# Attention with a linear feed-forward: the products of probabilities and values, key blocks in another order

## The chip, the cores and the metric

The kernel runs on one core of a Trainium2 chip. TensorE (PE) multiplies, VectorE (DVE) and ScalarE (ACT) work on what it leaves in PSUM, GpSimd (POOL) does little here, and SyncE (SP) issues DMAs. The metric is the device time of one execution in microseconds (us); lower is better.

## The reference

Attention over 4 batches, 8 heads, 768 positions and heads of 64, followed by a feed-forward without a nonlinearity:

```python
scores = scale * np.matmul(q, k.transpose(0, 1, 3, 2))
keep = is_global | is_local        # key < 8, or 0 <= query - key < 96
scores = np.where(keep, scores + bias, -1000000000.0)
a = np.exp(scores - np.max(scores, axis=-1, keepdims=True))
a = a / (np.sum(a, axis=-1, keepdims=True) + 1e-09)
attn = np.matmul(a, v)
...
h = (x @ w1) * (x @ w2) @ w3       # x: attn, heads side by side
out = h @ w_out
```

A query sees the 8 first keys and the 96 behind it, so the scores are a narrow band.

## The kernel before, in words

The attention part goes in 24 steps of 128 queries of one batch (`s`), for all eight heads at once, and two steps make a pair (`d`, 12 of them, three to a batch). Within a step the queries are cut into four groups of 32 (`R`); four pairs of heads (`hp`) lie at 32 rows each. For a step, PE multiplies queries and keys into `sc` in PSUM (`scores`, L963), DVE adds the bias and takes the maximum (`maxima`), ACT takes exponentials (`exponentials`), DVE divides by the sums (`scale_part`) and transposes the probabilities into `pt` (`turn`, L1013). The transposes of the even step of a pair come first, then those of the odd one, in the early pairs in one piece for each step, later in two halves.

When both steps of a pair are there, `values(d)` (L1016 to 1027) multiplies the probabilities with the values (`vr`). It goes over key blocks `i` of 32 keys, 12 for a pair (9 where the pair begins a batch, since the first three would lie before the batch). A key block meets the query groups whose band holds it: blocks 0 to 11 meet 1, 2, 3, 4, 5, 5, 5, 5, 4, 3, 2, 1 groups of 32 queries, so the products have 32 to 160 columns. A block has 8 products, one for each head: four pairs of heads in four groups of 32 rows of the array, and two heads of a pair in two groups of 64 columns. All is in float32, and each product is two weight loads (of the 32 x 64 values) and two matmuls on PE, which the profile counts apart. All blocks of a pair add into the same place in `sc`. `start` is set on the first block and `stop` on the last.

Blocks 0 to 3 read only probabilities of the even step of the pair, block 4 is the first to read the odd step's first group, block 6 the first that needs the odd step's second half.

The order of PE's work is the order in which the code issues it. The first eight steps stand in a list written out by hand (`ORDER`, V.0 to V.3 are `values(0)` to `values(3)`), the rest in `planned` and the loop behind it, which lays pieces of the feed-forward (the list `plan`) between the pieces of attention; `values(d)` is called there whole, but for pair 10, which is called in two pieces, blocks 0 to 7 and 8 to 11 (`CUT`). So a stage of values is a closed run on PE, with feed-forward matmuls before and behind it. The feed-forward goes on for 130 us after the last pair, in split products of seven multiplications.

Of the kernel before, what the change touches and what calls it, by code (L numbers as in the profile page):

```python
# [30 lines left out]
R = 32  # L31
NR = P // R
# [5 lines left out]
NB = S // P  # L38
NV = 3 * NR
# [19 lines left out]
PREPARED = (3, 1), (3, 5), (3, 6), (3, 2), (3, 7), (3, 4), (6, 1), (6, 5), (6, 6), (6, 7), (7, 1), (7, 5), (6, 4)  # L59
WIDE_AT = (2, 4), (2, 5), (2, 6), (2, 7), (3, 0), (3, 4), (3, 5)  # L60
CUT = 8
SHARED = 12
QUIET = 18, 104
LATER, HELD = (15,), (18,)
# [745 lines left out]
def strided(ap, *dims):  # L810

    return bass.AP(ap.tensor, ap.offset, [ap.ap[0], *dims])
# [15 lines left out]
def banded(ctx, tc, ff, ns, nt, n1, nf, oki, qk, vx, sc, pr):  # L828


    nc = tc.nc
# [23 lines left out]
    late, masked = [], []  # L855
# [109 lines left out]
    def maxima(s, q):  # L965

        if q == 0:
            stats[s] = [at.tile([P, NR, 2], F32, tag=t, bufs=2, name=f"{t}_{s}") for t in ("mx", "sm")]
        w0, w1 = frame(s, q)
        for u in range(2):  # L970
            bias = (biasw if s % NB else bias0)[:, u, q, w0:w1]
            nc.vector.tensor_tensor_reduce(out=pr[:, q, u, GLB + w0:GLB + w1], in0=scored(s, u, q, w0, w1), in1=bias, scale=-SCALE, scalar=3.0e38, op0=ALU.add, op1=ALU.min, accum_out=stats[s][0][:, q, u:u + 1])  # L972
# [42 lines left out]
    def values(d, first=0, end=NV):  # L1015


        pt, v = pts[d], vrs[d]
        i0 = 0 if d % (NB // 2) else NR - 1
        for i in range(max(i0, first), end):  # L1020
            n0, n1 = max(0, i - NR), min(2 * NR, i + 1)
            for hp in range(NP):
                rows = slice(hp * R, (hp + 1) * R)
                for u in range(2):
                    cols = slice(u * D, (u + 1) * D)
                    turned = strided(pt[rows, i * P + u * PF + n0 * (2 * PF - P):], [2 * PF - P, n1 - n0], [1, R])
                    nc.tensor.matmul(sc[cols, hp, n0 * R:n1 * R], lhsT=v[rows, i, cols], rhs=turned, start=i == i0, stop=i == NV - 1, skip_group_check=True)  # L1027

# [144 lines left out]

    units, homes, later, raws = {}, {}, {}, []
    do = dict(pj=ff.join, bo=ff.blocks_out, ps=ff.combine, sh=ff.sums_high, sl=ff.sums_low, so=ff.sums_out, A=lambda *x: ff.convert(0, *x), B=lambda *x: ff.convert(1, *x), C=lambda *x: ff.convert(2, *x), wh=ff.high, wl=ff.low, F=ff.fold, Y=lambda f: ff.fold_first(f, sc), ye=lambda f: ff.fold_begun(f, sc), ya=ff.fold_sum, pe=ff.fold_out, ph=ff.fold_high, pl=ff.fold_low, S=scores, R=maxima, E=exponentials, s=sums, c=lambda s: scale(s, nc.scalar if s in BY_ROWS else nc.vector), X=turn, V=values, h=high, l=low, bias=distances, bD=masks, bE=globals_near, biasA=biases, nt=sizes)
    do.update((name, lambda *x, method=method: getattr(units[0], method)(*x)) for name, method in (("U", "first"), ("a", "gate"), ("g", "product"), ("gh", "high"), ("gl", "low"), ("Z", "second"), ("ot", "store")))

# [113 lines left out]
    with tc.manual_schedule(engines={mybir.EngineType.PE}):  # L1293
        with tc.manual_schedule(engines={mybir.EngineType.DVE, mybir.EngineType.SP, mybir.EngineType.Activation, mybir.EngineType.Pool}):
            ordered()
        with tc.manual_schedule(engines={mybir.EngineType.Activation, mybir.EngineType.DVE}):
# [6 lines left out]
            def go(until):  # L1303
                for _, *todo in plan[done[0]:until]:
                    (_, call, *x), *rest = todo
                    call(*x)
                    for call, x in waiting:
                        call(*x)
                    waiting.clear()
                    for late, call, *x in rest:  # L1310
                        if late:
                            waiting.append((call, x))
                        else:
                            call(*x)
                done[0] = max(done[0], until)
                if done[0] == len(plan):
                    for call, x in waiting:
                        call(*x)
                    waiting.clear()

            def on(k):
                go(done[0] + k)

            def rows(s, paces, begun=False):
                if not begun:
                    maxima(s, 0)
                    if s >= SHARED:
                        on(1)
# [35 lines left out]
            for d in range(STEPS // 2, PAIRED):  # L1364
                load(d)
                for s in (2 * d + 2, 2 * d + 3):
                    keys(s)
                for s in (2 * d, 2 * d + 1):
                    rows(s, (1,) * NR)
                    first = d % 2 == 0 and s % 2 == 0  # L1370
                    on(2 if first else 0 if s % 2 else 3)
                    rest(s, 2 if first else 1)
                    if s % 2 == 0:
                        on(1 if first else 2)
                go(place["Z", 1, 2, 6] if d % 2 else place["U", 1, 4, 1, 1])
                values(d)
                tokens(d)
                go(place["Z", 1, 3, 2] if d % 2 else place["Z", 1, 0, 0])
                scores(2 * d + 2)
                scores(2 * d + 3)  # L1380
            start = place["Z", 1, 3, 2]
            with tc.manual_schedule(engines={mybir.EngineType.SP}):
# [5 lines left out]
                for d in range(PAIRED, n // 2):  # L1388
                    when, cut, gap = MEET[d][:3]
                    for s in (2 * d, 2 * d + 1):  # L1390
                        rows(s, MEET[d][3 + s % 2], s % 2 == 1)
                        on(1)

                        def middle():
                            if d > PAIRED and s % 2 == 0:
                                scores(s + 1)
                                if d < n // 2 - 1:
                                    keys(s + 3)

                        shared(s, middle)  # L1400
                        if s % 2 == 0:
                            on(1)
                    go(start + when)
                    values(d, 0, CUT if cut else NV)
                    if cut:
                        on(cut)
                        values(d, CUT)
                    if d < n // 2 - 1:
                        load(d + 1)
                    ff.release()  # L1410
                    tokens(d)
                    go(start + when + cut + gap)
                    if d < n // 2 - 1:
                        scores(2 * d + 2)
                        if d < n // 2 - 2:
                            keys(2 * d + 4)
# [44 lines left out]
```

## Time and profile before

| | |
|---|---|
| median of 3 runs | 503.88 us (503.84 to 504.58) |
| the profiled execution | 504.05 us, span 502.3 us |
| PE busy (matmuls) | 496.8 us, 99% of the span |
| DVE, ACT busy | 378.5 us (75%), 250.9 us (50%) |
| granted TensorE clock | 1.00 |
| line 1027 (the change's matmuls) | 2112 matmuls, from 47.0 to 372.0 us |

A matmul's end is modelled in the profile and runs over the next one's start, so a busy PE can still have gaps in its streaming. The time of a stage is read from its first matmul to the first matmul of what follows. The number behind an x in a stretch of the profile counts every matmul or weight load that is under way somewhere in the stretch; with a stretch that begins just before a stage, it is the number that have started up to the stretch's end.

### The profile page before, as it was taken

How to read it: one execution, taken by the hardware profiler on the slowest of the kernel's cores; microseconds unless marked ns; L12 is line 12 of the kernel's file. 1: busy time of each engine (PE TensorE's matmuls, PEld its weight loads, DVE VectorE, ACT ScalarE, POOL GpSimd, SP SyncE). 2: the span in 40 equal slices, each digit the busy share in tenths (PEclk: the TensorE clock that was granted, in tenths of full speed). 3: DMA queues.
4: the chain of work that ended last, by engine and by line, in shares of the span. 5: the costliest groups of instructions: out<-in, count | busy, mean ns of one | idle time of the engine just before them, and what ended most of it. 6: DMA issues, size and time to landing. Idle time of an engine off the chain costs nothing.

```text
span 502.3 us, 14240 instructions
## 1 busy us (share of the span) xinstructions
PE 496.8 (99%) x5920; PEld 407.3 (81%) x5920; DVE 378.5 (75%) x941; ACT 250.9 (50%) x730; POOL 3.8 (1%) x29
## 2 busy tenths in 40 slices
PE   8999999999999999999999999999999999999997
PEld 5445568888888888889999889999888888888997
DVE  7999989999997984958585757685867566367971
ACT  7148637454544543548474757564654211243641
POOL 3000000000000000000000000000000000000000
PEclk9999999999999999999999999999999999999999
DMA  8997906994869979468582346691112764000112
GB/s 314 417 369 286 386 22 198 374 346 145 309 205 383 301 246 350 159 228 269 211 330 67 124 135 221 194 404 57 60 44 77 206 199 127 21 2 0 43 44 89
DMA packets 39498, 99.96 MB, mean 199 GB/s; under 512 B 3458, under 2 KB 22658, under 8 KB 38274
## 3 DMA queue, kind: packets, MB, share of 16 engines
q1 hardware_dynamic: 39280, 98.84, 56.2%
q8 instruction: 48, 0.79, 0.6%
q14 instruction: 24, 0.20, 0.1%
q10 hardware_dynamic: 146, 0.13, 0.1%
HBM read 75.89 MB, written 23.07 MB: 197 GB/s over the span
## 4 chain that ended last, share of the span: by engine, by line
PE 98%; DVE 1%; ACT 0%; issue 0%; ACTq 0%
PE x L436 18%; PE y L436 11%; PE w L288 11%; PE o L369 7%; PE o L371 7%; PE o L370 7%; PE sc L1027 6%; PE m L336 6%; PE m L338 6%; PE m L337 6%; PE sc L963 4%; PE oy L636 3%; PE ox L636 2%; PE sc L436 2%; PE sc L636 1%; PE sc L296 1%
## 5 line engine op out<-in xcount | busy, mean ns | idle before, releaser
L979 ACT ACTIVATE pr<-pr,mx 128x136 f32<-128x136 f32 (+2 forms) x192 | 74.6, 391 | 35.2 <-DVE mx L972 35.0
L461 ACT ACTIVATE ag<-x 128x256 f32<-128x256 f32 (+1 forms) x48 | 21.8, 453 | 67.0 <-PE x L436 61.8
L369 PE MATMUL o<-wh,gh 128*128 128x512 f32 x128 | 51.4, 401 | 0.0
L371 PE MATMUL o<-wh,gl 128*128 128x512 f32 x128 | 50.0, 390 | 0.0
L370 PE MATMUL o<-wl,gh 128*128 128x512 f32 x128 | 49.9, 390 | 0.0
L336 PE MATMUL m<-xh,w12h 128*128 128x512 f32 x112 | 43.9, 392 | 0.0
L338 PE MATMUL m<-xh,w12l 128*128 128x512 f32 x112 | 43.6, 389 | 0.0
L337 PE MATMUL m<-xl,w12h 128*128 128x512 f32 x112 | 43.6, 389 | 0.0
L972 DVE CUSTOM_DVE_ANT_0 pr<-sc,biasw 128x136 f32<-128x136 f32 x144 | 34.7, 294 | 6.2 <-PE sc L963 5.1
L1013 DVE STREAM_TRANSPOSE pt<-pr 128x640 f32<-128x640 f32 (+1 forms) x37 | 38.3, 1037 | 0.6
L979 ACT ACTIVATION_READ_ACCUMULATOR pr<-pr,mx 128x1 f32 x192 | 36.3, 189 | 0.0
L1027 PEld LDWEIGHTS sc<-pt,vr 32*64 32x64 f32 x2112 | 30.6, 130 | 4.4 <-issue 1.8
L436 PE MATMUL x<-xh,w12h 128*128 128x256 f32 (+1 forms) x152 | 33.5, 302 | 0.0
L436 PE MATMUL x<-xh,w12l 128*128 128x256 f32 (+1 forms) x152 | 33.3, 301 | 0.0
L1027 PE MATMUL sc<-pt,vr 32*64 32x160 f32 (+4 forms) x2112 | 32.4, 266 | 0.0
L288 PE MATMUL w<-wo,kt 128*128 128x512 f32 x64 | 28.4, 597 | 0.9 <-DVE wo L208 0.9
L436 PE MATMUL x<-xl,w12l 128*128 128x256 f32 (+1 forms) x96 | 29.2, 318 | 0.0
L436 PE MATMUL x<-xl,w12h 128*128 128x256 f32 (+1 forms) x96 | 29.2, 318 | 0.0
L369 PEld LDWEIGHTS o<-wh,gh 128*128 128x128 f32 x128 | 24.0, 188 | 5.8 <-issue 0.8
L371 PEld LDWEIGHTS o<-wh,gl 128*128 128x128 f32 x128 | 24.0, 188 | 5.3
L436 PEld LDWEIGHTS x<-xh,w12h 128*128 128x128 f32 x152 | 26.1, 190 | 1.8 <-issue 0.4
L370 PEld LDWEIGHTS o<-wl,gh 128*128 128x128 f32 x128 | 24.1, 188 | 4.1
(287 smaller groups left out, 1134.4 us busy)
## 6 DMA issues: line engine op xcount, KB each, us to landing
qr<-qk SPq DMA_DIRECT2D x20, 720.0 KB, 6.9
w12h<-ws SPq DMA_DIRECT2D x16, 512.0 KB, 5.7
w12l<-ws SPq DMA_DIRECT2D x16, 512.0 KB, 5.8
vr<-vx SPq DMA_DIRECT2D x8, 768.0 KB, 4.8
w12h<-ws SPq DMA_DIRECT2D x8, 768.0 KB, 6.2
w12l<-ws SPq DMA_DIRECT2D x8, 768.0 KB, 7.4
out_dram<-ot SPq DMA_DIRECT2D x19, 256.0 KB, 2.4
raws<-w SPq DMA_DIRECT2D x4, 1024.0 KB, 7.8
```

The lines of the kernel that those rows point to most:

```text
L288: self.nc.tensor.matmul(self.prod[f], lhsT=block.bitcast(F32), rhs=self.wo[:, k].bitcast(F32), start=first, stop=k == NFC - 1)
L336: self.nc.tensor.matmul(ps, lhsT=mh, rhs=xh[:, i], start=i == 0, stop=False)
L337: self.nc.tensor.matmul(ps, lhsT=mh, rhs=xl[:, i], start=False, stop=False)
L338: self.nc.tensor.matmul(ps, lhsT=ml, rhs=xh[:, i], start=False, stop=i == NCC - 1)
L369: self.nc.tensor.matmul(ps, lhsT=gh, rhs=ff.wh[:, f], start=f == first, stop=False)
L370: self.nc.tensor.matmul(ps, lhsT=gh, rhs=ff.wl[f], start=False, stop=False)
L371: self.nc.tensor.matmul(ps, lhsT=gl, rhs=ff.wh[:, f], start=False, stop=f == last)
L436: self.nc.tensor.matmul(out, lhsT=w[:, i], rhs=x[:, i], start=fresh and i == 0 and j == 0, stop=i == 1 and j == 2, skip_group_check=True)
L972: nc.vector.tensor_tensor_reduce(out=pr[:, q, u, GLB + w0:GLB + w1], in0=scored(s, u, q, w0, w1), in1=bias, scale=-SCALE, scalar=3.0e38, o ...
L979: nc.scalar.activation(x, x, AF.Exp, bias=mx[:, q, u:u + 1], scale=-1.0, accum_out=sm[:, q, u:u + 1])
L1013: nc.vector.transpose(strided(pts[d][:, (half * NR + q0) * 2 * PF:], [PF, 2 * (q1 - q0)], [P, NR + 1], [1, R]), x.rearrange("p n (k c) -> ...
L1027: nc.tensor.matmul(sc[cols, hp, n0 * R:n1 * R], lhsT=v[rows, i, cols], rhs=turned, start=i == i0, stop=i == NV - 1, skip_group_check=True)
```

## The change

The key blocks of a pair are visited in an order that is written out, one for full pairs, one for the pairs that begin a batch, and one for pair 4 (`LATE_TURN`). In widths (units of 32 columns) they are 5 1 5 2 4 3 5 1 5 2 4 3 for full pairs, 4 5 5 5 1 5 2 4 3 for those that begin a batch, and 4 1 3 2 5 5 5 1 5 2 4 3 for pair 4. Pair 10, which is cut, has 5 1 5 2 4 3 5 5 and then 1 2 4 3. `start` and `stop` follow the first and the last block of the order.

```diff
+LATE_TURN = 4
+ORDERS = {"full": (4, 0, 5, 1, 3, 2, 6, 11, 7, 10, 8, 9), "late": (3, 0, 2, 1, 4, 5, 6, 11, 7, 10, 8, 9), "first": (3, 4, 5, 6, 11, 7, 10, 8, 9)}
...
         pt, v = pts[d], vrs[d]
-        i0 = 0 if d % (NB // 2) else NR - 1
-        for i in range(max(i0, first), end):
+        order = [i for i in ORDERS["first" if d % (NB // 2) == 0 else "late" if d == LATE_TURN else "full"] if first <= i < end]
+        for i in order:
             n0, n1 = max(0, i - NR), min(2 * NR, i + 1)
...
-                    nc.tensor.matmul(sc[cols, hp, n0 * R:n1 * R], lhsT=v[rows, i, cols], rhs=turned, start=i == i0, stop=i == NV - 1, skip_group_check=True)
+                    nc.tensor.matmul(sc[cols, hp, n0 * R:n1 * R], lhsT=v[rows, i, cols], rhs=turned, start=i == order[0] and first == 0, stop=i == order[-1] and end == NV, skip_group_check=True)
```

On PE, pair 1 (the stage at 67.40 us in the trace of before) stands in the kernel before as follows; a row is a run of products of one width (64 partitions of output by so many columns), `pt_715` are its transposed probabilities and `vr_708` its values:

```order
L1027 MATMUL sc<-pt_715,vr_708 64x32 x8
L1027 MATMUL sc<-pt_715,vr_708 64x64 x8
L1027 MATMUL sc<-pt_715,vr_708 64x96 x8
L1027 MATMUL sc<-pt_715,vr_708 64x128 x8
L1027 MATMUL sc<-pt_715,vr_708 64x160 x32
L1027 MATMUL sc<-pt_715,vr_708 64x128 x8
L1027 MATMUL sc<-pt_715,vr_708 64x96 x8
L1027 MATMUL sc<-pt_715,vr_708 64x64 x8
L1027 MATMUL sc<-pt_715,vr_708 64x32 x8
```

And in the changed kernel, where the line is 1029:

```order
L1029 MATMUL sc<-pt_715,vr_708 64x160 x8
L1029 MATMUL sc<-pt_715,vr_708 64x32 x8
L1029 MATMUL sc<-pt_715,vr_708 64x160 x8
L1029 MATMUL sc<-pt_715,vr_708 64x64 x8
L1029 MATMUL sc<-pt_715,vr_708 64x128 x8
L1029 MATMUL sc<-pt_715,vr_708 64x96 x8
L1029 MATMUL sc<-pt_715,vr_708 64x160 x8
L1029 MATMUL sc<-pt_715,vr_708 64x32 x8
L1029 MATMUL sc<-pt_715,vr_708 64x160 x8
L1029 MATMUL sc<-pt_715,vr_708 64x64 x8
L1029 MATMUL sc<-pt_715,vr_708 64x128 x8
L1029 MATMUL sc<-pt_715,vr_708 64x96 x8
```

The run of four blocks of 160 columns is broken up, and every block of 32 or 64 columns now lies between wider ones. Pair 0, which begins a batch (the stage at 46.96 us), stands in the changed kernel so:

```order
L1029 MATMUL sc<-pt_448,vr_465 64x128 x8
L1029 MATMUL sc<-pt_448,vr_465 64x160 x24
L1029 MATMUL sc<-pt_448,vr_465 64x32 x8
L1029 MATMUL sc<-pt_448,vr_465 64x160 x8
L1029 MATMUL sc<-pt_448,vr_465 64x64 x8
L1029 MATMUL sc<-pt_448,vr_465 64x128 x8
L1029 MATMUL sc<-pt_448,vr_465 64x96 x8
```

Here only the last 160-column block and what followed it have moved: before, it was 128, four times 160, then 128, 96, 64 and 32. The instructions of DVE, ACT, POOL and SP stand as before.

## Rows read from the trace of the kernel before

**Rows 1.** The page: busy time of each engine, and the chain that ended last.
```profile
PE 496.8 (99%) x5920; PEld 407.3 (81%) x5920; DVE 378.5 (75%) x941; ACT 250.9 (50%) x730; POOL 3.8 (1%) x29
PE 98%; DVE 1%; ACT 0%; issue 0%; ACTq 0%
```

**Rows 2.** PE in order of time: start, length, instructions merged under the first shape.
```profile
67.40 2.82 PE L1027 MATMUL sc<-pt,vr 32*64 32x32 f32 x192
70.15 0.70 PE L288 MATMUL w<-wo,t 128*128 128x512 f32 x1
```

**Rows 3.** The chain of waits in order of time: start, length, what.
```profile
142.91 2.26 PE sc L1027 x127
...
268.20 2.91 PE sc L1027 x165
...
344.68 2.05 PE sc L1027 x118
...
349.08 0.95 PE sc L1027 x52
```

**Rows 4.** Line 1027, stretches from 142.80: PE matmuls, PE weight loads (x), clock, DMA.
```profile
142.80:143.01 0.21, 0.17 (x9) 0.17 (x16) 1.00 0.17 54
142.80:143.30 0.50, 0.46 (x32) 0.46 (x33) 1.00 0.07 23
142.80:143.31 0.51, 0.47 (x32) 0.47 (x34) 1.00 0.07 22
142.80:143.39 0.59, 0.55 (x33) 0.55 (x40) 1.00 0.06 19
142.80:144.07 1.27, 1.23 (x73) 1.23 (x81) 1.00 0.03 9
142.80:144.20 1.40, 1.35 (x80) 1.36 (x86) 1.00 0.03 8
142.80:144.32 1.52, 1.48 (x90) 1.48 (x97) 1.00 0.02 7
142.80:144.39 1.59, 1.54 (x96) 1.55 (x97) 1.00 0.02 7
142.80:144.41 1.61, 1.56 (x96) 1.57 (x99) 1.00 0.02 7
142.80:144.61 1.81, 1.76 (x112) 1.77 (x115) 1.00 0.02 6
142.80:144.80 2.00, 1.96 (x128) 1.96 (x132) 1.00 0.02 6
142.80:144.97 2.17, 2.12 (x144) 2.13 (x144) 1.00 0.03 9
```

**Rows 5.** Line 1027, stretches from 67.39, the same columns.
```profile
67.39:67.68 0.29, 0.28 (x32) 0.28 (x33) 1.00 0.00 0
67.39:67.72 0.33, 0.32 (x33) 0.32 (x34) 1.00 0.00 0
```

**Rows 6.** Line 1027's matmuls in three stretches: ns min/median/max, first and last start, forms.
```profile
L1027 PE MATMUL sc<-pt,vr x40: 294/294/318, 143.2 to 143.9; 32*64 32x160 f32 x40
...
L1027 PE MATMUL sc<-pt,vr x8: 318/318/319, 142.8 to 142.9; 32*64 32x128 f32 x8
...
L1027 PE MATMUL sc<-pt,vr x42: 217/238/315, 67.4 to 67.8; 32*64 32x32 f32 x16, 32*64 32x64 f32 x16, 32*64 32x96 f32 x9, 32*64 32x128 f32 x1
```

**Rows 7.** Line 1027, stretches from 268.10, columns as in rows 4.
```profile
268.10:269.41 1.31, 1.28 (x95) 1.28 (x96) 1.00 0.00 0
268.10:269.53 1.43, 1.40 (x96) 1.28 (x96) 1.00 0.00 0
```

**Rows 8.** DVE in order of time: the odd steps' transposes ahead of three stages.
```profile
65.72 1.51 DVE L1013 STREAM_TRANSPOSE pt<-pr 128x1280 f32<-128x1280 f32 x1
...
175.28 1.51 DVE L1013 STREAM_TRANSPOSE pt<-pr 128x1280 f32<-128x1280 f32 x1
...
266.98 0.85 DVE L1013 STREAM_TRANSPOSE pt<-pr 128x640 f32<-128x640 f32 x1
```

## The prediction

> **What bounds the kernel now.** I read the page first. TensorE (PE) is busy for 99% of the span and the chain of waits is PE for 98% [rows 1], so what the stages of this change gain or lose on PE reaches the end, unless a wait elsewhere takes it. Next I looked at the stages of line 1027 alone. There are twelve, one for each pair of steps, and three kinds. Pairs with all twelve key blocks take 2.75 us up to the next stage's first matmul (six of them: 67.40 to 70.15 [rows 2]; a seventh takes 2.91). Pairs that begin a batch have nine blocks and take 2.26 (four). One pair is cut in two, 2.05 and 0.95 [rows 3]. Together that is 31.4 us.
>
> Then I looked into a stage. A block is 8 products, and each product is two weight loads and two matmuls, so a block is 32 instructions of PE. A 160-column block behind a 160-column block costs 0.27 us: the 33rd matmul of the stage at 142.84 starts by 143.39, the 81st just after 144.20, three blocks in 0.81 us. That is two passes of 0.135 on each of 8 parts of the array, 0.027 us a pass for 32 columns: PE streams without a gap there. Narrow blocks don't: in the same stage the 81st, 97th, 113th and 129th matmul start at about 144.20, 144.42, 144.61 and 144.80 [rows 4], so the blocks of 128, 96 and 64 columns take 0.22, 0.19 and 0.19, where streaming alone would be 0.22, 0.16 and 0.11. So a full stage of 40 x 0.054 = 2.16 us of streaming has some 0.6 us on top, and the question is what sets it.
>
> **Reading the limit.** Three rows say that it is not the weight loads as such. At the start of the stage at 67.40, 32 matmuls (32 pairs of load and matmul, 64 instructions) start within 0.28 us, at 0.009 a pair, weight loads included; then PE pauses, and the 33rd comes by 67.72 [rows 5]. So 64 instructions, two blocks, are at hand at a time. When does the next one come in? In the stage at 142.84 the 9th matmul (the leading product's second pass, block 1) starts by 143.01 and lasts 0.27 (a 160-column one lasts 0.294, less 0.027 for 32 columns fewer [rows 6]), so it ends at 143.27; the 34th weight load, which belongs to the second product of block 3, comes between 143.30 and 143.31. In the tail, the 73rd matmul (second pass of the leading product of the last 160-column block) starts by 144.07 and ends at 144.36; the weight loads stand at 97 from 144.32 to 144.39 and go on by 144.41, with the block after next [rows 4]. Both times the load follows 0.03 after the end of a product two blocks back. The rule I take from this: **a block's loads wait for the end of the products of the block before the last**, in program order. From load to streaming it is 0.05: the first eight matmuls of a stage, which wait for their weights, last 0.318, and a 128-column one that doesn't lasts 0.267 [rows 6].
>
> That gives a price for a step over two blocks. Behind a leading block of 160 columns: one pass 0.135, the second pass's duration 0.294, 0.03, 0.05, together 0.51 us. For 128 columns 0.11 + 0.267 + 0.08 = 0.455, for 96 it is 0.08 + 0.24 + 0.08 = 0.40. Where both blocks are 160 wide, streaming needs 0.54 and the step is hidden. Where the block between is narrow, it is not: it decides for every neighbour narrower than 160. The tail checks it: 128 to 64 takes 0.41 and 96 to 32 takes 0.38 by the first matmul of each block, 0.045 and 0.02 under my sums, since that leading product enters one product earlier than the rest. I take a third of the larger difference off: 0.495, 0.44 and 0.385.
>
> [...]
>
> **The change part by part.** Nothing is added or removed: the same 1056 products with the same operands, only in another order within a stage; other engines keep their order. In the new order nearly every wide block has a narrow one behind it, so the pair streams in 0.32 to 0.38 (six or seven times 0.054) and costs the step of the wide one, 0.495 (0.44 for 128 and 96).
> Full order (widths in units of 32: 5 1 5 2 4 3 5 1 5 2 4 3): 0.05 for the first load, four steps of 0.495 and one of 0.44, then the last two blocks: 0.22 for the 4, 0.08 for the first pass of the 3, 0.12 until the last of 8 products has started (7 x 0.27/16), and 0.17 until the next stage's first matmul. That last is the duration of a 96-column matmul, 0.24, less 0.07, since the next stage begins 0.07 before the recorded end of this one (70.15 against 67.40 + 2.82 [rows 2]). These last four are 0.59. Sum 3.06 against 2.75: +0.31, five times, 1.55.
> The seventh full stage (268.13) today stops at its seventh block for DVE's last transpose: PE's count stands from 269.41 to 269.53 [rows 7]. The new order puts the same amount of work before that block, and by the sum it is reached 1.48 us in, behind the 1.40 at which the data are there; so its wait of 0.13 goes and it loses only 3.06 - 2.91 = 0.15.
> Late order (4 1 3 2 5 5 5 1 5 2 4 3): 0.05 + 0.44 + 0.385 + two streamed 160-blocks 0.54 + 0.99 + 0.59 = 3.0, +0.25.
> First order (4 5 5 5 1 5 2 4 3): 0.81 streamed as today, 0.99 + 0.59 = 2.39 against 2.26, +0.13, four times, 0.52.
> The cut pair: 5 1 5 2 4 3 5 5 is 0.05 + 0.99 + 0.44 + 0.27 + 0.135 + 0.12 and a run-out of 0.22 (0.294 - 0.07), 2.22 against 2.05, +0.17; in its second piece, 1 2 4 3, both narrow blocks come out of the 64 instructions at hand and the 4 follows the 1 by a step of about 0.33 (0.385 for 96 columns, less 0.027 for each 32 fewer): 0.05 + 0.33 + 0.59 = 0.97 against 0.95, +0.02.
> Sum: 1.55 + 0.15 + 0.25 + 0.52 + 0.17 + 0.02 = +2.66 us.
>
> What else the order moves: the first block of a full stage now needs the odd step's transposes, where it needed only the even step's. The spare time is small but there: at 67.40 the transpose ended at 65.72 + 1.51 = 67.23; at 268.13 the half that is needed ended at 266.98 + 0.85 = 267.83 [rows 8]. At the fifth pair it would not be there (175.28 + 1.51 = 176.79, stage from 176.23), and there the late order starts with four blocks that don't need it; by my sum they take 0.05 + 0.44 + 0.385 = 0.88, to 177.1. As PE gets later at each stage, none of this cover shrinks; I cost it at nothing. If DVE slipped as much as PE, it would be up to 0.1 a stage, inside my range.
>
> **Range of the steps.** From below: all steps by the smaller measured difference, 0.045 less than the sum (0.465, 0.41, 0.355). Then the full stage is 2.91 (+0.16), the seventh level, late +0.13, first +0.07, cut +0.08: +1.3. From above, the undiminished sums: 3.14 (+0.39), +0.23, +0.31, +0.16, +0.22: +3.3. The profiled execution took 504.05, 0.17 over the median of the runs shown, 503.88. On the median I get 506.5, and put the forecast at 506.6, in its own range of 505.2 to 507.3.
>
> **The rivals.** (a) The loads are what costs, and a wide block hides those of a narrow one. For it: narrow blocks run over their streaming time, in the tail by up to 0.08 us. Against it: at a stage's start 32 pairs go out at 0.009 us each with 32- and 64-column blocks, and the pause comes after the 64th instruction, not with the narrow block. If so, a full stage is 0.05 + 40 x 0.054 - 0.08 + 0.12 + 0.17 = 2.42, -0.33 (six times, with the late one), the seventh -0.2, because its wait for DVE stays, the first ones -0.16 each, the cut pair -0.25: -3.1. Of this about 0.6 comes back as waits for transposes at the heads, whose spare is 0.1 to 0.3. That gives 501.4; it decides from the point where a narrow block's loads don't need the end of a block two back. [...]
> (b) A block costs what its own width costs, whatever its neighbours. For it: the 160-blocks are alike everywhere. Then the order moves only the ends: 0.02 more run-out behind a 96- than a 32-column block, twelve times, +0.2: 504.1. Against it: the blocks of 64 and 32 columns take 0.36 together in the tail (144.61 to 144.97 [rows 4]) and 0.28 at a stage's start [rows 5].
>
> **How the numbers follow.** My forecast 80%, (a) 11%, (b) 9%. A measurement of this kernel tells 0.2%, 1.0 us, from no change. My own case lies over that bound whole (from 504.9), (b) within it, (a) below: faster 0.12, same 0.09, slower 0.79. The range takes in (b) and leaves out (a): 504.0 to 507.5.
>
> **What would show it.** In the changed profile full stages of 3.0 to 3.1 us, first ones of 2.35 to 2.45, and no wait in the stage near 268; within a stage, weight loads that stand still while a narrow block has run out, and starts of wide blocks 0.46 to 0.51 apart. It would be wrong if a narrow block behind a wide one took its streaming time and the next wide one followed at once, or if PE stood at the stages' heads for DVE.

## The result and the profile after

The changed kernel takes 509.06 us (median, 508.62 to 509.42), the kernel before 504.23 us beside it: 1.0095 times as long, 95% interval 1.0077 to 1.0112, +4.8 us. The forecast was 506.6 in a range of 504.0 to 507.5, so the direction was right and the time lies over the range. The profiled execution took 508.62 us with a span of 506.8, 4.5 over that of before.

The page shows what answers to [rows 1]: PE as busy as before, and now two groups of the changed line (1029 here) whose idle time is put down to "issue". The second row is the queue that brings instructions: packets, MB, share of 16 engines.

```profile
PE 499.9 (99%) x5920; PEld 409.0 (81%) x5920; DVE 378.9 (75%) x941; ACT 250.6 (49%) x730; POOL 3.8 (1%) x29
...
q8 instruction: 48, 0.79, 0.6%
...
PE 98%; DVE 1%; issue 0%; ACT 0%; ACTq 0%
...
L1029 PEld LDWEIGHTS sc<-pt,vr 32*64 32x64 f32 x2112 | 32.8, 131 | 6.2 <-issue 3.3
L1029 PE MATMUL sc<-pt,vr 32*64 32x160 f32 (+4 forms) x2112 | 36.2, 267 | 1.0 <-issue 0.9
```

Idle time before the stages' matmuls is new (1.0 us against 0.0, 0.9 of it "issue", time in which PE waited for nothing that the profile names); before their weight loads "issue" has grown from 1.8 us to 3.3. The chain of waits says where, in answer to [rows 3] (start, length, what; from seven places of the program):

```profile
67.35 2.43 PE sc L1029 x92
69.78 0.87 issue
70.65 1.01 PE sc L1029 x34
...
120.25 3.07 PE sc L1029 x123
...
144.66 2.40 PE sc L1029 x112
...
216.33 2.44 PE sc L1029 x93
218.78 0.12 issue
218.90 0.95 PE sc L1029 x37
...
271.25 3.48 PE sc L1029 x123
...
348.76 2.24 PE sc L1029 x95
...
353.34 0.95 PE sc L1029 x56
```

Pair 2 (120.25) takes 3.07 us, a pair that begins a batch (144.66) 2.40, the cut pair 2.24 and 0.95: the prediction had 3.06, 2.39, 2.22 and 0.97. But pair 1 shows 0.87 us of "issue" in its middle, pair 5 0.12, and pair 7 takes 3.48. By the starts of their matmuls these three stages take 4.31, 3.51 and 3.48 us where pairs 2, 8 and 11 take 3.07: 2.09 us in all that no term of the prediction's sum has.

A stage without a stop, pair 2 (line 1029 alone, in answer to [rows 4]; PE matmuls and weight loads with their counts in brackets, clock, DMA; the last row, in answer to [rows 6], gives the matmuls that have started by 121.00 by their columns):

```profile
120.14:120.65 0.51, 0.47 (x33) 0.47 (x34) 1.00 0.00 0
120.14:121.14 1.00, 0.96 (x65) 0.96 (x68) 1.00 0.00 0
120.14:121.20 1.06, 1.02 (x67) 1.02 (x68) 1.00 0.00 0
...
L1029 PE MATMUL sc<-pt,vr x51: 187/294/345, 120.2 to 121.0; 32*64 32x160 f32 x32, 32*64 32x32 f32 x16, 32*64 32x64 f32 x2, 32*64 32x128 f32 x1
```

The count of weight loads stands at 68 from 121.14 to 121.20, while two matmuls start. The last row shows that neighbouring blocks mix: the block of 128 columns has begun when only two matmuls of the 64 columns ahead of it have, so the count of matmuls does not tell where a block begins. By their columns, the five wide blocks behind the first one (the left ones of the pairs in 5 1, 5 2, 4 3, 5 1, 5 2, 4 3) begin 0.41, 0.83, 1.34, 1.74 and 2.23 us into the stage, 0.40 to 0.52 apart. That is the step over two blocks.

Pair 1, in answer to [rows 2] and [rows 8], all engines in order of time (idle time before a row in brackets, with what ended it):

```profile
65.60 1.51 DVE L1015 STREAM_TRANSPOSE pt<-pr 128x1280 f32<-128x1280 f32 x1
...
67.28 2.22 PEld L1029 LDWEIGHTS sc<-pt,vr 32*64 32x64 f32 x142 [0.76 <-DVE pt L1015]
67.28 2.50 PE L1029 MATMUL sc<-pt,vr 32*64 32x160 f32 x141
...
70.65 1.01 PE L1029 MATMUL sc<-pt,vr 32*64 32x160 f32 x51 [0.87 <-issue]
70.65 0.82 PEld L1029 LDWEIGHTS sc<-pt,vr 32*64 32x64 f32 x50 [1.15 <-issue]
```

The odd step's transposes end at 67.11 (65.60 + 1.51), and the stage begins at 67.28 with a wide block that needs them: the wait costs nothing itself, as I had reckoned. But 2.2 us in, PE stops until 70.65 with nothing to wait for. What came in that time is on the DMA (all engines' busy time, clock, DMA share, GB/s):

```profile
67.20:68.20 1.00, 1.00 (x60) 0.93 (x66) 0.97 (x2) 0.00 (x0) 0.00 (x0) 1.00 0.00 0
68.20:68.30 0.10, 0.10 (x29) 0.10 (x11) 0.10 (x1) 0.00 (x0) 0.00 (x0) 1.00 0.66 164
69.78:70.64 0.86, 0.00 (x0) 0.00 (x0) 0.86 (x2) 0.00 (x0) 0.00 (x0) 1.00 0.00 0
```

Nothing is moved from 67.20 to 68.20, then 16.4 KB (164 GB/s in 0.1 us), then nothing. 16.4 KB is one packet of the instruction queue: 0.79 MB in 48. PE's 11,929 instructions in 48 packets are some 249 each; and counted in PE's stream, the three stops come before its 1473rd, 5057th and 6849th instruction, which are 14 x 256 and 7 x 256 apart. So code arrives in blocks of 256 instructions, and PE stood for one. (1472 instructions are 5 x 256 + 192, so a block does not begin with the first instruction that the trace shows; "a multiple of 256" means from here on a place in the stream that is a whole number of blocks away from these three.) The packet of pair 1 starts 0.95 us behind the stage's head, its first matmul; in the trace of before, that for the same place starts 3.96 us ahead of it. For pair 5 it is 0.23 behind against 0.84 ahead, for pair 7 0.49 ahead against 1.96. In all three PE goes on 2.37 to 2.42 us after the packet's start. In the kernel before, pair 1's packet lies in the first of these stretches, and in its whole stage nothing is moved (clock, DMA share, GB/s):

```profile
63.30:63.60 0.30, 1.00 0.47 170
...
67.20:70.20 3.00, 1.00 0.00 0
```

### The profile page after: what moved, and what is told of

It is laid out like the page before. It is cut to its first block, busy times and chain, and to the rows that moved or that the text cites. A ratio compares the mean times of both kernels' runs of the same rounds, so it can differ in the third digit from the quotient of the medians.

```text
span 506.8 us, 14243 instructions
## 1 busy us (share of the span) xinstructions
PE 499.9 (99%) x5920; PEld 409.0 (81%) x5920; DVE 378.9 (75%) x941; ACT 250.6 (49%) x730; POOL 3.8 (1%) x29
## 4 chain that ended last, share of the span: by engine, by line
PE 98%; DVE 1%; issue 0%; ACT 0%; ACTq 0%
PE x L438 18%; PE y L438 11%; PE w L290 10%; PE sc L1029 7%; PE o L371 7%; PE o L372 6%; PE o L373 6%; PE m L338 6%; PE m L340 6%; PE m L339 6%; PE sc L965 4%; PE oy L638 3%; PE ox L638 2%; PE sc L438 2%; PE sc L638 1%; PE sc L298 1%
## 5 line engine op out<-in xcount | busy, mean ns | idle before, releaser
L1029 PEld LDWEIGHTS sc<-pt,vr 32*64 32x64 f32 x2112 | 32.8, 131 | 6.2 <-issue 3.3
L1029 PE MATMUL sc<-pt,vr 32*64 32x160 f32 (+4 forms) x2112 | 36.2, 267 | 1.0 <-issue 0.9
L438 PEld LDWEIGHTS x<-xh,w12l 128*128 128x128 f32 x152 | 26.1, 191 | 1.6 <-issue 0.4
```

Of the source, the lines that this page charges most:

```text
L438: self.nc.tensor.matmul(out, lhsT=w[:, i], rhs=x[:, i], start=fresh and i == 0 and j == 0, stop=i == 1 and j == 2, skip_group_check=True)
```

## The experiments

All were timed beside the kernel before. "Behind the head" is how many PE instructions after a stage's first one a multiple of 256 falls (32 to a key block; the expectations of 3 and 4 count one more). A stop stands at the next multiple, 256 instructions later: in pair 1 of the changed kernel the multiple falls 26 behind the head, and PE stops after 282 instructions of the stage. Theory 1 was, to begin with: the order moves the wait for the odd step's transposes to the head of the stage, PE can't run ahead past it, so the next block of code is asked for late. The rival: the new order by itself, or the pace of the stage, causes the stops.

**1. The wide head taken away, the alternation left.** All full pairs take the order of pair 4, whose first four blocks need the even step alone.

```diff
-ORDERS = {"full": (4, 0, 5, 1, 3, 2, 6, 11, 7, 10, 8, 9), ...
+ORDERS = {"full": (3, 0, 2, 1, 4, 5, 6, 11, 7, 10, 8, 9), ...
```

> Full pairs begin with the blocks 3, 0, 2, 1, which need only the even step's transposes, and go on 4 5 6 11 7 10 8 9, so wide and narrow blocks still alternate in the second half. Theory 1 (part of the loss is the two-block step, the rest is code that comes late because the head of a full stage now waits for the odd step's transposes): every full stage takes 3.00 to 3.03 us, the stops of 1.2, 0.4 and 0.3 us inside the stages of pairs 1, 5 and 7 are gone, total about 506.6 us (ratio 1.005). Rival (the stops come from the alternation of wide and narrow blocks itself): stops of 0.3 us or more stay in the ninth blocks of these stages, total 508 to 509.

Measured: 506.29 us, ratio 1.0041 (1.0027 to 1.0055). Pair 1 on PE, with what follows it:

```profile
67.42 3.08 PE L1029 MATMUL sc<-pt,vr 32*64 32x128 f32 x192
70.43 1.98 PE L290 MATMUL w<-wo,t 128*128 128x512 f32 x4
```

3.01 us, as pair 4 and as predicted for this order (3.00), and no stop in any stage; the packet for pair 1 starts 3.86 us ahead of the head again. The steps alone cost some 2 us in this order; the stops of pairs 1, 5 and 7 are gone with the wide head.

**2. The head alone.** Full pairs start with block 4 and are ascending otherwise; the other pairs are as before.

```diff
+ORDERS = {"full": (4, 0, 1, 2, 3, 5, 6, 7, 8, 9, 10, 11), "late": (0, 1, ..., 11), "first": (3, 4, ..., 11)}
```

> Ascending order as before, but block 4 (160 columns, needs the odd step) is put at the head of every full pair; the other pairs are as before. Theory 1 (head waits, code comes late): by the two-block step a full stage costs 2.83 us, +0.09 each, +0.6 in all; the stops at a boundary of 256 instructions come back in pairs 1 and 5 with 0.4 to 1.3 us each, perhaps in pair 7; total 506.0 to 507.0. Rival (the stops come from the alternation itself): no stop, total 504.8.

Measured: 507.12 us, ratio 1.0063 (1.0043 to 1.0082), a little above the 506.0 to 507.0 expected. Pair 1:

```profile
67.15 2.38 PE L1029 MATMUL sc<-pt,vr 32*64 32x160 f32 x141
70.55 0.88 PE L1029 MATMUL sc<-pt,vr 32*64 32x128 f32 x51 [1.02 <-issue]
```

The stops of pairs 1 and 5 are there (4.21 and 3.37 us against 2.83 for the undisturbed ones), with the packets 0.97 and 0.34 us behind the heads. Pair 7 has none. So one moved block brings back 1.92 us of stops, of the 2.09 of the changed kernel, in an order that hardly alternates.

**3 and 4. The place of the multiples of 256.** The changed kernel with 16 more and 16 fewer warm-up matmuls at the program's start (32 instructions of PE), and nothing else:

```diff
-WARM = (24, 42)
+WARM = (24, 58)
```

> The changed kernel with 16 more warm-up matmuls at the start (32 more PE instructions), which moves every later PE instruction 32 places on against the blocks of 256 in which code is brought. In pairs 1 and 5 the boundary before the one at which PE stopped then lies 5 and 3 instructions ahead of the stage's head and no more 27 and 29 behind it. Theory 1: the code is asked for before the head's wait, the stops of pairs 1 and 5 (1.2 and 0.4 us) go, total 507.3 to 507.8 with up to 0.3 us for the warm-up. Rival (the stops belong to the products): they stay at the same products, total 509.

Measured: 508.79 us, ratio 1.0092 (1.0069 to 1.0114): not below the changed kernel, so the expected time was missed. The stops of pairs 1, 5 and 7 are gone (3.07 us each), but pair 8 has a new one:

```profile
293.09 2.98 PE L1029 MATMUL sc<-pt,vr 32*64 32x160 f32 x183
297.29 0.40 PE L1029 MATMUL sc<-pt,vr 32*64 32x96 f32 x9 [1.22 <-issue]
```

It comes after 366 instructions, where a multiple of 256 falls; the one before falls at 110, and the packet starts 1.48 us into the stage. Then fewer warm-ups:

```diff
-WARM = (24, 42)
+WARM = (24, 26)
```

> The changed kernel with 16 fewer warm-up matmuls (32 fewer PE instructions). Theory 1: PE stops 32 instructions later in the stage of pairs 1 and 5 (behind 315 instead of 283 instructions of the stage), and a stop can appear in pairs 2 and 11, where the boundary moves from 11 and 2 instructions behind the head to 43 and 34; total 509 to 511. Rival (the stops belong to the products): the stops stay at the same products, behind 283 to 285 instructions of the stage, total 509.

Measured: 515.76 us, ratio 1.0217 (1.0195 to 1.0238), far over the expected time. Two places of PE's timeline:

```profile
7.42 4.63 PE L290 MATMUL w<-wo,kt 128*128 128x512 f32 x5 [1.49 <-DVE wo L210]
...
221.34 2.63 PE L1029 MATMUL sc<-pt,vr 32*64 32x160 f32 x158
225.74 0.66 PE L1029 MATMUL sc<-pt,vr 32*64 32x64 f32 x34 [1.77 <-issue]
```

Stops stand in pairs 1, 2, 3, 5 and 11, 0.5 to 2.0 us each, 32 instructions later in the stage than before where they were there already. And 2.9 us are lost at the start: the first eight matmuls of 512 columns take 6.57 us, where the changed kernel's take 3.70. They start 0.85 us apart or more up to 12.70 and 0.43 apart from 13.39 on, as in the changed kernel. The record of the granted clock in this trace begins only at 13.2 us, with the full grant; in the other eleven traces it begins between 4.7 and 7.5 us, in the changed kernel's at 4.8 (for a stretch ahead of the record a view prints 1.00 all the same). So up to there TensorE started these matmuls half as often, at a clock of which the trace has no record. Its warm-up had ended at 5.9 us, and it had stood for 1.49 us. The rest of the loss, some 1.4 us, lies between the stages, 0.75 of it in a wait for DVE at 115 us.

That a stop moves with the count of instructions, by the same 32, settles that it is code. But the new stop in pair 8 says that the head's wait is not all. So the same shifts were made in the kernel before, whose heads need the even step alone.

**5. The kernel before with 16 more warm-ups**, the edit of experiment 3 in ascending order:

```diff
-WARM = (24, 42)
+WARM = (24, 58)
```

> The kernel before, in ascending order, with 16 more warm-up matmuls (32 more instructions of PE) at the start, so that the multiples of 256 instructions fall 32 instructions earlier in every stage, as in the third experiment. Theory 1 (a stop needs a head at which PE waits for the odd step's transposes, since PE then cannot fetch ahead): no stop over 0.15 us in any stage; the warm-up shifts the first stage by 0.45 us, of which some may be lost later; 504.2 to 505.0. Rival (a stop needs only that the next multiple but one of 256 falls inside the stage and that the stage uses up 256 instructions faster than 2.4 us): as in the third experiment the eighth pair's stage has a multiple some 112 instructions behind its head and the next at 368; reached some 2.6 us in, with the block there some 3.85 us in: one stop of 1.0 to 1.4 us at about 291, 505.5 to 506.5.

Measured: 505.91 us, ratio 1.0026 (1.0017 to 1.0036). Pair 8:

```profile
291.40 2.75 PE L1027 MATMUL sc<-pt,vr 32*64 32x32 f32 x184
295.31 0.32 PE L1027 MATMUL sc<-pt,vr 32*64 32x32 f32 x8 [1.17 <-issue]
```

The rival's number: one stop (1.38 us between two matmuls), after 368 instructions, packet 1.47 us behind the head. Theory 1, that a stop needs a waiting head, is wrong as a general statement: where a multiple falls far behind the head and the next inside the stage (112 and 368 here, 110 and 366 in experiment 3), PE had used up the 256 instructions between them before the packet was of use, in either order: from its start to PE's next matmul it took 2.44 us here and 2.72 there.

**6. The kernel before with 32 instructions fewer**, the warm-up's streaming kept (50 matmuls of 128 columns for 66 of 96):

```diff
-WARM = (24, 42)
+WARM = (18, 32)
...
-            nc.tensor.matmul(y, lhsT=x[:, :P], rhs=x[:, :96], start=True, stop=True)
+            nc.tensor.matmul(y, lhsT=x[:, :P], rhs=x[:, :P], start=True, stop=True)
```

> The kernel before, in ascending order, with 16 warm-up matmuls fewer but each of 128 columns in place of 96 (50 of them, the streaming as before), so 32 instructions fewer and the multiples of 256 fall 32 instructions later in every stage, as in the fourth experiment. Theory 1 (the wait at the head holds back the next block of instructions): no stop over 0.15 us in pairs 1, 2, 3, 5 and 11, 503.8 to 505.0. Rival (the place of the multiples and the speed of the stage alone): stops in pairs 1, 2, 5 and 11 as in the fourth experiment, 0.7 to 2 us each, 507 to 509.

Measured: 511.68 us, ratio 1.0151 (1.0133 to 1.0169), above both expectations. Pair 1, and its DMA:

```profile
67.23 2.48 PE L1027 MATMUL sc<-pt,vr 32*64 32x32 f32 x157
70.90 0.59 PE L1027 MATMUL sc<-pt,vr 32*64 32x96 f32 x35 [1.20 <-issue]
```

```profile
67.23:68.10 0.87, 0.87 (x74) 0.87 (x80) 0.83 (x2) 0.00 (x0) 0.00 (x0) 1.00 0.00 0
68.10:68.30 0.20, 0.20 (x30) 0.20 (x23) 0.20 (x1) 0.00 (x0) 0.00 (x0) 1.00 0.35 82
68.30:69.40 1.10, 1.10 (x87) 1.10 (x76) 1.07 (x2) 0.00 (x0) 0.00 (x0) 1.00 0.00 0
```

An ascending stage whose head doesn't wait for the odd step stops like the changed one: the packet (16.4 KB at 68.1) starts 0.96 us behind the head. The multiples lie 58, 43 and 61 behind the heads of pairs 1, 2 and 5, which stop for 1.44, 1.16 and 1.70 us; 36 behind that of pair 11, whose packet starts 0.59 us ahead and which doesn't stop. Pair 3 stops too, for 0.30 us, though a multiple falls just ahead of its head: its packet starts 0.05 us behind the head. The kernel before comes to 511.7 us by a shift of 32 instructions. In the profiled execution (510.09 us) the span is 6.0 us longer: 4.6 of it are in the four stages that stop, and 1.2 in a wait for DVE at 113 us, for which no run gives the cause.

**7. The changed kernel with the same warm-up as 6**, its 128 columns included:

```diff
-WARM = (24, 42)
+WARM = (18, 32)
...
```

> The changed kernel with the same warm-up as the sixth experiment: the fourth experiment without its loss of streaming at the start. If the fourth experiment's first 2.9 us were the clock (its first eight matmuls of 512 columns took 6.57 us in place of 3.70), they are gone here, the stops in pairs 1, 2, 3, 5 and 11 stay (0.5 to 2 us each), 511.5 to 513.5. If the loss came from elsewhere, 514 to 516. If the stops of the fourth experiment hung on the time of the start and not on the place of the multiples of 256, they are gone too: 507 to 509.

Measured: 513.04 us, ratio 1.0156 (1.0131 to 1.0180), from 511.0 to 515.5; the trace is of the slowest.

```profile
7.42 3.70 PE L290 MATMUL w<-wo,kt 128*128 128x512 f32 x8 [0.48 <-DVE wo L210]
...
69.34 2.61 PE L1029 MATMUL sc<-pt,vr 32*64 32x160 f32 x157
72.86 0.71 PE L1029 MATMUL sc<-pt,vr 32*64 32x64 f32 x35 [0.90 <-issue]
```

The first eight matmuls take 3.70 us again, and the clock's record begins at 6.5 us with the full grant: experiment 4's 2.9 us hung on the warm-up's streaming, and the stops on the count. They are in pairs 1, 2, 3, 5 and 11 as there (0.5 to 1.7 us), and in pair 7 (0.40). One more, of 1.21 us, stands at 54.99 in the scores, at a multiple of 256 too, and the wait for DVE, at 114 us, is 1.57 here.

**8. Is it the step over two blocks?** Experiment 1's order (the line taken out is that of experiment 1), with the narrow blocks side by side:

```diff
-ORDERS = {"full": (3, 0, 2, 1, 4, 5, 6, 11, 7, 10, 8, 9), ...
+ORDERS = {"full": (3, 0, 1, 2, 4, 5, 6, 11, 10, 7, 8, 9), ...
```

> The first experiment's order with its narrow blocks in runs: widths 4 1 2 3 5 5 5 1 2 5 4 3 in place of 4 1 3 2 5 5 5 1 5 2 4 3 for all pairs that are not first in a batch. By the two-block rule (a block's loads wait for the end of the products of the block before the last), a wide block behind two narrow ones costs less, and a full stage takes 2.88 us against 3.01 there; no stops; 505.4 to 506.0. Rival (the same narrow blocks among wide ones cost the same in either grouping): 3.0 us, 506.2 to 506.7.

Measured: 505.78 us, ratio 1.0019 (1.0002 to 1.0037), 0.5 us below experiment 1 with the same blocks. Pair 2:

```profile
118.75 2.95 PE L1029 MATMUL sc<-pt,vr 32*64 32x128 f32 x192
121.62 0.50 PE L371 MATMUL o<-wh,gh 128*128 128x512 f32 x1
```

2.87 us to the next stage (2.88 expected, 3.01 in experiment 1), no stops. So the narrow blocks have no fixed price: one between two wide ones costs more than one beside another narrow one.

**9 and 10. What the head's wait does.** The changed kernel with 4 and with 8 more warm-ups, (24, 46) and (24, 50): the multiple falls 18 and 20, then 10 and 12 behind the waiting heads of pairs 1 and 5.

```diff
-WARM = (24, 42)
+WARM = (24, 46)
```

> The changed kernel with 4 more warm-up matmuls of 96 columns at the start (8 more instructions of PE), so the multiples of 256 instructions fall 8 earlier: in pairs 1 and 5 the first lies 18 and 20 behind the head in place of 26 and 28, in pair 7 190 in place of 198, in pair 8 the second 390 behind the head, which is just behind its 384. Theory (a waiting head holds the next packet back only where the multiple of 256 lies more than some 12 to 26 instructions behind it; 12 behind the head had no stop, 26 had): the stops in pairs 1, 5 and 7 go or shrink below 0.3 us, a new one of up to 0.6 us may stand just behind pair 8's stage; what is left is the steps alone, +2.7 us: 506.6 to 507.6. Rival (the stops come from the waiting head wherever the multiple lies): 1.2, 0.4 and 0.3 us stay, 508.5 to 509.2.

Measured: 509.04 us, ratio 1.0091 (1.0073 to 1.0109). Pair 1:

```profile
67.71 2.40 PE L1029 MATMUL sc<-pt,vr 32*64 32x160 f32 x137
70.95 1.13 PE L1029 MATMUL sc<-pt,vr 32*64 32x160 f32 x55 [0.84 <-issue]
```

The rival's numbers: 1.13 and 0.43 us stay in pairs 1 and 5 (pair 7's is gone, but the first stage begins 0.43 us later). My bound of 12 to 26 instructions held, but 18 is on its bad side.

And with 8 more:

```diff
-WARM = (24, 42)
+WARM = (24, 50)
```

> The changed kernel with 8 more warm-up matmuls (16 more instructions of PE): the first multiple of 256 lies 10 behind the head of pair 1 and 12 behind that of pair 5 (18 and 20 in the ninth experiment, where the stops stayed), the second multiple of pair 8 lies 382 behind its head, 2 ahead of the stage's end. Theory (the waiting head holds the packet back only from some 12 to 18 instructions on; with the multiple 10 to 12 behind waiting heads other pairs had their packet ahead of the head): no stop in pairs 1, 5 and 7, a stop of 0.8 to 1.2 us at the end of pair 8's stage; 507.5 to 508.6. Rival (pairs 1 and 5 stop wherever the multiple lies behind the head): 1.1 and 0.4 us stay there besides pair 8's, 509.0 to 510.2.

Measured: 508.17 us, ratio 1.0083 (1.0066 to 1.0100). Pairs 1 and 8:

```profile
67.27 3.14 PE L1029 MATMUL sc<-pt,vr 32*64 32x160 f32 x192
70.35 2.84 PE L290 MATMUL w<-wo,t 128*128 128x512 f32 x6
...
292.86 3.13 PE L1029 MATMUL sc<-pt,vr 32*64 32x160 f32 x191
296.93 0.24 PE L1029 MATMUL sc<-pt,vr 32*64 32x96 f32 x1 [0.95 <-issue]
```

Pair 1's stage on all engines, with clock, DMA share and GB/s:

```profile
67.27:69.80 2.53, 2.53 (x171) 2.53 (x171) 2.46 (x3) 0.00 (x0) 0.00 (x0) 1.00 0.00 0
```

With the multiple eight instructions earlier pair 1 has no stop, and nothing is moved in its stage: its packet starts 4.22 us ahead of the head in place of 0.81 behind; pair 5 likewise (2.91 ahead). What is left is 1.19 us in pair 8, after 382 instructions, as expected. Taken off, the span of 506.13 is 504.94, 2.69 above the 502.25 of before: the sum of the prediction.

Pairs 1, 2, 5 and 11, then, with heads that need the odd step's transposes ("waits") and heads that need the even step's alone (packet from the head, minus is ahead):

| kernel | pair | head waits | multiple behind the head | packet, us | stop, us |
|---|---|---|---|---|---|
| experiment 10 | 1, 5 | yes | 10, 12 | -4.22, -2.91 | none |
| experiment 9 | 1, 5 | yes | 18, 20 | +0.81, +0.07 | 1.13, 0.43 |
| changed | 1, 5 | yes | 26, 28 | +0.95, +0.23 | 1.17, 0.41 |
| before | 1, 5 | no | 26, 29 | -3.96, -0.84 | none |
| experiment 1 | 1, 5 | no | 26, 29 | -3.86, -0.94 | none |
| experiment 7 | 11 | yes | 33 | +0.90 | 1.04 |
| experiment 6 | 11 | no | 36 | -0.59 | none |
| experiment 6 | 2, 1, 5 | no | 43, 58, 61 | +0.98, +0.96, +1.05 | 1.16, 1.44, 1.70 |

In these pairs the packet starts ahead of the head where the multiple lies up to 36 behind a head that doesn't wait, and up to 12 behind one that does. In pairs 1 and 5 of the changed kernel the multiple lies between the two. Pair 3, the first of its batch, does not fit: its head needs the even step alone, the multiple falls 1 (experiment 6) or 2 (4 and 7) ahead of it, and yet the packet starts 0.05 to 0.18 us behind it and the stage stops for 0.30 to 0.53 us.

## Why the prediction was wrong, and where it was right

**What bounds the kernel**: right. PE is 99% busy, and what the stages gain or lose reaches the end. All stages together, each up to the next stage's first matmul, grew by 4.8 us, the span by 4.5.

**The step over two blocks**: right for the stages as wholes. Undisturbed stages take 3.07 (predicted 3.06), 2.39 (2.39), 3.01 (3.00), 2.24 and 0.95 (2.22 and 0.97). Summed without the stops the twelve pairs cost +2.75 against the +2.66 of the sum. Experiments 1, 2 and 8, with three other orders, came to the times that the rule gave (3.01, 2.83 and 2.88), and 8 tells it from a price for each narrow block. Inside a stage the terms are less exact, and that they cancel is luck: the five steps up to the last pair of blocks take 2.23 where I had 2.47 with the first load, and the rest 0.84 where I had 0.59; the wide blocks begin 0.40 to 0.52 apart where I had 0.46 to 0.51. One reading behind the steps was wrong: the 113th and 129th matmul of the stage at 142.84 are not the first of the blocks of 64 and 32 columns. By their columns these begin at 144.59 and 144.73, so 128 to 64 takes 0.38 and 96 to 32 takes 0.31, which is 0.07 and 0.09 under the sums, not 0.045 and 0.02.

**Pair 7's wait for DVE**: its old wait went as predicted, shown where no stop covers it (3.07 in experiments 3, 9 and 10); in the changed kernel a stop of 0.29 us took its place.

**The head**: this is the step that failed. "The first block of a full stage now needs the odd step's transposes ... I cost it at nothing" looked at one thing alone, whether the data are late, and they are not: the transposes end 0.17 us ahead of the head of pair 1 and 1.2 us ahead of that of pair 5. The bound "up to 0.1 a stage" is of the same kind. What the wait at the head also did is hold back the code behind it: pair 1's packet started 0.95 us behind the head, in the kernel before 3.96 us ahead of it. The three stops that came with the new order cost 2.1 us, near the whole difference between the sum and the measurement: 2.75 + 2.09 = 4.84 against the 4.8 measured. For pairs 1 and 5, 1.7 us of them, the head is shown as the cause: they go when it is taken away (experiment 1) and come back with it alone (2). For pair 7's 0.4 it is not shown: experiment 2 has the head and no stop there. And the head alone is not enough, it hangs on where the multiples of 256 fall: experiment 10 keeps the head and has no stop in any of the three.

**The rivals**: (a) and (b) are both out: no stage is shorter, and full stages without a stop are 0.32 us longer. The case that came true, steps and code stops together, wasn't among them; in the trace of before nothing stands still, but the packets of the instruction queue could have been seen, that of pair 5 only 0.84 us ahead of a stage that uses 256 instructions in 1.8 to 2.0 us.

Left open: what exactly sends a packet off. Counted through the whole trace of the changed kernel, one starts anywhere from 40 instructions ahead of a multiple to 171 behind it; pair 3, above, fits no bound. In pair 7, which stops at the multiple 198 behind a waiting head (the one before falls 58 ahead of the head), it started 0.49 us ahead of the head in the changed kernel, with a stop, and 1.41 ahead in experiment 2, with none; no run explains the difference. None of the ten beat the kernel before.

## What to carry to other kernels

A reordering that moves a wait to the front of a run of short instructions can cost though the wait itself is over in time: here the packet with the engine's next block of code then started later, in pair 1 0.95 us behind the head in place of 3.96 ahead of it, and PE stood for 1.17 us. Count the engine's instructions, look where the multiples of the block fall in such runs, and where idle time inside a run is put down to "issue", look at the times of the instruction queue's packets. And before a kernel is judged by a few microseconds, shift the count by a few instructions at the start: here 32 instructions fewer, with the warm-up's streaming kept, moved the kernel before by 7 us, more than the change under study.

## What the runs showed of the hardware

- PE's code came in blocks of 256 instructions (16.4 KB a packet; the changed kernel's three stops lie 14 x 256 and 7 x 256 instructions apart). From the start of a packet to PE's next matmul it took 2.2 to 3.1 us in the stages that stopped (3.14 in pair 5 of experiment 4); a stage of values without a stop uses 256 instructions in 1.8 to 2.1 us (traces of before and of the changed kernel). Where the packet for a multiple inside the stage started 0.05 to 1.6 us behind the head (the table, pairs 3 and 8), PE stopped for 0.30 to 1.70 us.
- No packet of these traces started more than 299 instructions, little over one block, ahead of its use: at most 43 instructions ahead of a multiple, for the code from the next multiple on. Where the multiple lies 110 to 126 behind pair 8's head, the packet started 1.5 to 1.6 us into the stage (experiments 3, 5 and 10).
- A matmul of this kernel may start before one that stands ahead of it in the program: in the changed kernel's pair 2 the first of 128 columns has started when two of the 16 of 64 columns ahead of it have. That a block's loads wait for the products of the block before the last is worked out from the trace of before and gave the stage times of experiments 1, 2 and 8 (3.01, 2.83, 2.88) within 0.01 us.
- After a warm-up of 50 matmuls of 96 columns, which ended at 5.9 us, and 1.49 us of standing still, the record of TensorE's clock, with the full grant (1.00), begins only at 13.2 us (experiment 4); with 50 of 128 columns it begins at 6.5 us, while these still ran (experiment 7). The first eight matmuls of 512 columns took 6.57 us in the one and 3.70 in the other.
